# Reordering the first two head pairs of an attention and feed-forward kernel, and splitting its first loads

## The chip, the cores and the metric

One core of a Trainium2 chip runs the whole program. The metric is the time of one execution on the device in microseconds (us); the lower, the better. The core has a matrix engine (PE, with its weight loads, PEld), a vector engine (DVE), an activation engine (ACT), a general engine (POOL) and a queue engine (SP) that here does nothing but issue transfers. Transfers from HBM run on 16 DMA engines that all queues share.

## The reference

The inputs are q, k and v for 4 batches of 8 heads, 576 positions and 64 features. The reference adds two attentions and passes the result through two feed-forward blocks:

```python
q_d, k_d, v_d = means over groups of 4 positions        # 144 positions
out_up = repeat(softmax(q_d @ k_d.T / 8) @ v_d, 4)
scores = where(abs(i - j) < 4, q @ k.T / 8, -1e9)
x = out_up + softmax(scores) @ v                        # then (4, 576, 512)
xn = (x - mean(x)) / sqrt(var(x) + 1e-6) * g_ln
x = x + maximum(xn @ w_ch1, 0) @ w_ch2                  # 512 -> 2048 -> 512
xk, xr = mixes of x and x shifted by one position
out = sigmoid(xr @ w_r) * (square(maximum(xk @ w_k, 0)) @ w_v)
```

The weights reach the kernel as 64-bit words and are decoded to f32 on the core. Each product is made from three products of rounded halves (high by high, high by low, low by high).

## The kernel before

The 2304 tokens are cut into 6 chunks of 384. A chunk goes through attention (4 units, each of two heads), the norm, and the first feed-forward block. While PE runs the block of chunk c, the attention of chunk c+1 is fed in between by a budget. The second feed-forward block follows over all chunks. The change touches only the start: the attention of chunk 0 and the loading and decoding of the first weights.

**Chunk 0's attention** is done for two pairs of units at once. `pair(0)` and `pair(1)` are generators, and the string `FIRST` (L1339) is the order, written out by hand, in which their steps and a few others are emitted. Every instruction in it is held in program order on its engine. A `0` or `1` makes the next step of that pair. The steps of a pair are, in order:

1. sums of q and k over groups of four (DVE)
2. score products (PE, L861 and L868)
3. row maxima of the coarse scores (DVE, L879) and their exponentials (ACT, L884)
4. minimum with the mask, row maxima, subtraction (DVE, L887 to L889), exponential (ACT, L890)
5. row sums, reciprocals, scaling (DVE, L892 to L896)
6. transposes of the local part (DVE, L898) and scaling of the coarse part (ACT, L902)
7. copies of the transposed tile (L906: ACT; for the second pair two of them on DVE)
8. transposes of the coarse part (PE, L912), copies of them (ACT, L914), then `busy(IDLE)` for the first pair only
9. value products (PE, L923 and L930)
10. sum of the two attentions into x (ACT L939, DVE L940)
11. the mean over features (PE, L953)

The other letters: `a` and `b` are `value_sums` of the first and second pair (DVE, L792 and L794), which adds four loaded rows of v into one and is needed by step 9; `A`, `D`, `H` and `L` with a number decode and split that weight tile (A: two passes on ACT, L80 and L81; D: one on DVE, L83; H: the high half, ACT, L86; L: the low half, DVE, L89); `.` is `busy(1)` (L366), a matrix product whose result nobody uses; `W` is the same with `WARM` products (L360); `n` is the norm. After `FIRST`, `emit_first` (L680) makes the first four column blocks of the first layer, which needs weight tiles 0 and 1. Tiles 2 and 3 belong to the second layer. From tile 4 on, the planner orders the decoding.

**The loads** of the start are issued in program order: q and k of pair 0, q and k of pair 1 (some from ACT's queue), mask, vector; then `load_pair_v(0)` (L783) and `load_pair_vr(0)` (L788), the v windows and v rows of the first pair in one transfer each; then the first weight tile (L122: two transfers of 128 rows by 4 KB, 512 KB each); the coarse sums' first rows of the next units (L336, L337); the second pair's v rows, weight tile 1, the second pair's v windows, weight tile 2, q and k of the next two units (L313, L317), weight tile 3 and the next v (L322). Each later weight tile is asked for when an earlier one is decoded (step D). The program has eight semaphores for the transfers of SP and ACT together and takes them in turn, so that the ninth transfer in program order can be issued only when the first has landed, the tenth when the second has, and so on.

Of the kernel before, what the change touches and what calls it, by code (L numbers as in the profile page):

```python
# [22 lines left out]
NG = 4  # L23
# [4 lines left out]
KD = SD // 2  # L28
# [10 lines left out]
def tile_block(ctx: ExitStack, tc: tile.TileContext, qw, kw, kf, kr, vw, vr, vec, mask, w1, w2, wk, wv, wr, out):  # L39
    nc = tc.nc  # L40
# [27 lines left out]
    def in_order(on, ins):  # L68
        if on:
            tc.keep_in_program_order(ins)  # L70
# [5 lines left out]
    def decode(raw, pinned, ru):  # L76

        low, high = (raw.rearrange("p (n t) -> p n t", t=2)[:, :, i] for i in range(2))
        top = raw.bitcast(U8).rearrange("p (n t) -> p n t", t=8)[:, :, 3]
        in_order(pinned, nc.scalar.activation(ru.bitcast(F32), high.bitcast(F32), AF.Prelu, scale=-2.0 ** -80, alpha=-2.0 ** -32))  # L80
        in_order(True, nc.scalar.activation(low, top, AF.Copy, scale=1.0 / 32.0, bias=-31.0 / 64.0))  # L81
        yield ru.bitcast(F32)
        in_order(pinned, nc.vector.scalar_tensor_tensor(ru, ru, 3, low.bitcast(U32), op0=ALU.logical_shift_left, op1=ALU.bitwise_or))  # L83

    def split_hi(hi, w, vector=False):
        return nc.vector.tensor_copy(hi, w) if vector else nc.scalar.copy(hi, w)  # L86

    def split_lo(hi, lo, w):
        return nc.vector.tensor_tensor(lo, w, hi.bitcast(F32), op=ALU.subtract)  # L89

    def wtiles(nm):
        return [wpool.tile([128, 4, 512], F32R, tag="w", name=f"{nm}{t}") for t in "hl"]
# [7 lines left out]
    def pieces_w12():  # L100
        for p in range(3):
            yield from ((nm, p, k, 2) for nm in ("w1", "w2") for k in (0, 2))
        yield from ((nm, 3, k, 1) for nm in ("w1", "w2") for k in range(4))

    def conv_gen():
        keys = list(pieces_w12())
        late_keys = keys[-4:]
        raws, todo = {}, iter([(nm, p, k) for nm, p, k, _ in keys[:-4] if k % 2 == 0])

        def source(nm, p, k):  # L110
            return w1s[:, k, 1024 * p:1024 * p + 1024] if nm == "w1" else w2s[:, 4 * p + k, :]

        def fetch():
            key = next(todo, None)
            if key is None:
                return
            nm, p, k = key
            t = wpool.tile([128, 2, 1024], I32, tag="w", name="raw")
            raws[nm, p, k, 2] = t.rearrange("p k n -> p (k n)")
            for i in range(2):  # L120
                raws[nm, p, k + i, 1] = t[:, i]
                in_order(len(raws) < 12, nc.sync.dma_start(t[:, i], source(nm, p, k + i)))  # L122

        def fetch_late(key):
            if key in late_keys:
                t = raws[key] = stg.tile([128, 1024], I32, tag="stg", name="raw", bufs=RB)
                nc.sync.dma_start(t, source(*key[:3]))

        parts, got = {}, set()

        def step(op, n):

            if not 0 <= n < len(keys) or (op, n) in got:
                return
            got.add((op, n))
            pin = n < PINNED
            nm, p, k, m = keys[n]
            W = W1 if nm == "w1" else W2
            if op == "A":
                if p not in W:  # L140
                    W[p] = wtiles(f"{nm}_{p}")
                if m == 1:
                    rm = stg.tile([128, 2, 512], U32, tag="stg", name="rm", bufs=RB)[:, 0]
                elif k == 0:
                    parts["rm"] = wpool.tile([128, 2, 1024], U32, tag="w", name="rm")
                    rm = parts["rm"][:, 0]
                else:
                    rm = parts["rm"][:, 1]
                g = decode(raws[keys[n]], pin, rm)
                parts[n] = (g, next(g), *(t[:, k:k + m, :].rearrange("p k n -> p (k n)") for t in W[p]))  # L150
                return
            g, w, h, l = parts[n]
            if op == "D":
                next(g, None)
                if m == 2 or k % 2:
                    fetch()
                if n + 1 < len(keys):
                    fetch_late(keys[n + 1])
            elif op == "H":
                in_order(pin, split_hi(h, w, n in BY_VECTOR))  # L160
            else:
                in_order(pin, split_lo(h, l, w))
                done.update((nm, p, k + i) for i in range(m))

        for _ in range(AHEAD):
            fetch()
            yield
        yield step
        for n in range(len(keys) + 1):
            for ops in ((("H", n - 1), ("A", n)), (("L", n - 1), ("D", n))):  # L170
                if all(not 0 <= i < len(keys) or (op, i) in got for op, i in ops):
                    continue
                for op, i in ops:
                    step(op, i)
                yield
# [186 lines left out]
    def busy(n):  # L362

        for _ in range(n):
            bank = ps_at.tile([128, 512], F32, tag="sc", name="idle")
            in_order(True, nc.tensor.matmul(bank, ident, sets[0]["kf"][:, 0, 0:512], start=True, stop=True))  # L366
# [378 lines left out]
    def block(*parts):  # L745

        t = wpool.tile([128, 2048], F32, tag="w", name="first")
        n, views = 0, []
        for m in parts:
            views.append(t[:, n:n + m])  # L750
            n += m
        return views
# [9 lines left out]
    sets = [  # L762
        dict(q=q_0, kf=kf_0, qd=qd_0, v=v_0, Pd=pd_0, PdT=td_0, P=P_both, PT=pt_0, T=t_0),
        dict(q=q_1, kf=kf_1, qd=qd_1, v=v_1, Pd=pd_1, PdT=td_1, P=p_1.rearrange("p (g w) -> p g w", w=32), PT=pt_1, T=t_1),
    ]
# [14 lines left out]
            in_order(True, (nc.sync if pr else nc.scalar).dma_start(b["kf"][:, i], kf[0, 2 * pr + i]))  # L780

    def load_pair_v(pr):
        in_order(True, nc.sync.dma_start(sets[pr]["v"], vw[2 * pr:2 * pr + 2, :, 0:NG].rearrange("i p n h d -> p i n h d")))  # L783

    vr_01 = [block(2048)[0].rearrange("p (i r f) -> p i r f", i=2, r=4) for _ in range(2)]

    def load_pair_vr(pr):
        in_order(True, nc.sync.dma_start(vr_01[pr][0:KD].rearrange("p i r f -> p i (r f)"), vr[0, 2 * pr:2 * pr + 2].rearrange("i p r t d -> p i (r t d)")))  # L788

    def value_sums(pr):  # L790
        t = vr_01[pr][0:KD]
# [16 lines left out]
    nc.scalar.copy(ones_r, one)  # L808
    make_identity(nc, ident)
    load_pair_v(0)  # L810
    load_pair_vr(0)
    next(conv)
    for h in range(2):
        p = slice(64 * h, 64 * h + 64)
# [6 lines left out]
    for _ in zip(*[sums(*units[NHP + i]) for i in range(2)]):  # L821
        pass
    load_pair_vr(1)
    next(conv)
    load_pair_v(1)
    next(conv)
    for i in range(2):
# [13 lines left out]
    def pair(pr):  # L841
# [71 lines left out]
        for i in both:  # L913
            fixed(nc.scalar.copy(  # L914
                PdT[0:KD, i].rearrange("p t j (h m) -> p (t j) h m", h=2),
                tp[i].rearrange("p t j (h m) -> p (t j) h m", h=2)[:, :, :, 0:QB]))
        busy(0 if pr else IDLE)
        yield
# [37 lines left out]
    def first_norm():  # L956

        mean = means.pop(0)
        xc = xct[0] = pln.tile([128, KT, N], F32, tag="xc", name="xc")
        for k in range(KT):  # L960
            in_order(True, nc.vector.tensor_tensor(xc[:, k, :], xt[0][:, k, :], mean[:, 0:N], op=ALU.subtract))
        yield
        yield from split_x(0, True)
# [4 lines left out]
    steps = {"0": pair(0), "1": pair(1), "n": first_norm()}  # L968
    for o in FIRST.split():
        if o in "ab":  # L970
# [179 lines left out]
    def small(nm, tag="s", bufs=None):  # L1150
        return (right if tag == "k" else left)[-1].tile([128, N], F32, tag=tag, name=nm, bufs=bufs or SB)
# [94 lines left out]
    for s in range(NSC):  # L1246
# [28 lines left out]
        for j in range(2):  # L1275
            for o in range(KT):
                ps = bank()
                c = slice(128 * o, 128 * o + 128)
                n = slice(N * j, N * j + N)
                for k in range(KT):  # L1280
                    mm3(ps[:, 0:N], wr_t[0][:, k, c], wr_t[1][:, k, c], xh[:, k, n], xl[:, k, n], k == 0, k == KT - 1)
                t = small("r")
# [18 lines left out]
    for c in range(NCH):  # L1301
# [5 lines left out]
        for o in range(KT):  # L1307
# [6 lines left out]
            r = rins[c][o]  # L1314
# [21 lines left out]
PROB = 800  # L1336
PRO0 = 10
GAP = -1
FIRST = "0 0 1 1 0 0 1 . . A0 0 0 1 0 a 0 1 1 1 0 b 0 D0 1 H0 1 0 1 1 L0 A1 n n D1 H1 W n L1 A2 D2 H2 L2 A3 D3"  # L1339
EARLY = 44  # L1340
IDLE = 2
WARM = 8


# [55 lines left out]
```

## Time and profile before

| | |
|---|---|
| median of 3 runs | 749.43 us (748.63 to 751.29) |
| profiled execution: its time | 749.87 us |
| profiled execution: its span, first to last instruction | 748.1 us |
| PE busy | 733.1 us, 98% of the span |
| DVE, ACT, POOL busy | 439.1 us (59%), 374.5 us (50%), 106.5 us (14%) |
| bytes moved | 130.43 MB, 174 GB/s over the span |

The busy shares are means over stages. The start, some 100 us, has other limits than the rest: there DVE, ACT and the transfers are loaded as heavily as PE. The rows below are therefore taken from that stretch.

### The profile page before, as it was taken

The numbers are of one execution on the slowest core, as the hardware profiler recorded it, in microseconds if no ns is written. First come the engines' busy times: TensorE is split into PE (matmuls) and PEld (weight loads), VectorE is DVE, ScalarE is ACT, GpSimd is POOL, SyncE is SP. The second block draws the span as 40 slices with busy tenths as digits, with TensorE's granted clock in tenths as the row PEclk, the third lists the DMA queues.
The fourth block names the chain that finished last, engine by engine and source line by source line (L and its number), as shares of the span: only waits on it lengthen the run. The fifth ranks groups of instructions, "written<-read, shape, count | busy, mean of one in ns | idle before, by whom it ended". The sixth has DMA issues, their size and how long they took to land.

```text
span 748.1 us, 14134 instructions
## 1 busy us (share of the span) xinstructions
PE 733.1 (98%) x5548; PEld 707.5 (95%) x5548; DVE 439.1 (59%) x820; ACT 374.5 (50%) x781; POOL 106.5 (14%) x141
## 2 busy tenths in 40 slices
PE   6899999999999999999999999999999999999997
PEld 5598899999999999999999999999999999999997
DVE  5889977755475657555766455447997266233211
ACT  2798884653353543444454444236987476311100
POOL 3431203200164205410300030002000000000000
PEclk9999999999999999999999999999999999999999
DMA  8999552646366745754432247807725637785311
GB/s 266 263 345 361 108 172 76 173 139 204 100 172 159 184 142 141 193 159 129 137 122 93 77 142 271 292 29 262 236 83 188 221 103 301 259 281 168 109 67 47
DMA packets 75354, 130.43 MB, mean 174 GB/s; under 512 B 8376, under 2 KB 51896, under 8 KB 73624
## 3 DMA queue, kind: packets, MB, share of 16 engines
q1 hardware_dynamic: 64792, 119.57, 48.8%
q0 software_dynamic: 9920, 9.25, 6.9%
q8 instruction: 43, 0.70, 0.4%
q10 hardware_dynamic: 576, 0.72, 0.3%
q14 instruction: 23, 0.19, 0.1%
HBM read 89.13 MB, written 40.37 MB: 173 GB/s over the span
## 4 chain that ended last, share of the span: by engine, by line
PE 89%; DMA 8%; ACT 1%; DVE 0%; issue 0%; SPq 0%; ACTq 0%
PE b_ps L1189 12%; PE acc L291 9%; PE h_ps L291 9%; PE acc L292 8%; PE acc L293 8%; PE h_ps L292 8%; PE h_ps L293 8%; PE b_ps L291 7%; PE b_ps L293 7%; PE b_ps L292 7%; DMA raw<-in_w 3%; PE av L476 2%; DMA q<-in_qw 2%; DMA first<-in_vr 2%; PE sc L404 1%; DMA v<-in_vw 1%
## 5 line engine op out<-in xcount | busy, mean ns | idle before, releaser
L670 ACT ACTIVATE hh<-h_ps 128x384 fp32r<-128x384 f32 x96 | 47.0, 489 | 102.9 <-PE h_ps L293 101.1
L671 DVE SCALAR_TENSOR_TENSOR hl<-h_ps,hh 128x384 fp32r<-128x384 f32 x96 | 53.1, 553 | 76.8 <-ACT hh L670 76.2
L1189 PE MATMUL b_ps<-xk,wk 128*128 128x384 f32 x504 | 87.9, 334 | 0.0
L1189 PEld LDWEIGHTS b_ps<-xk,wk 128*128 128x128 f32 x504 | 87.5, 188 | 0.0
L713 POOL TENSOR_TENSOR x<-x2t,x 128x384 f32<-128x384 f32 x24 | 24.1, 1020 | 291.1 <-DVE x2t L712 290.9
L291 PE MATMUL b_ps<-ko,wv 128*128 128x384 f32 x192 | 64.1, 334 | 0.0
L293 PE MATMUL b_ps<-ko,wv 128*128 128x384 f32 x192 | 64.1, 334 | 0.0
L292 PE MATMUL b_ps<-ko,wv 128*128 128x384 f32 x192 | 64.1, 334 | 0.0
L1315 DVE TENSOR_TENSOR rin<-b_ps,rin 128x384 f32<-128x384 f32 x24 | 13.3, 557 | 61.9 <-PE b_ps L293 61.1
L336 POOL DMA_DIRECT2D kd<-in_kr x36 | 35.3, 982 | 85.4 <-DMA kd<-in_kr 76.1
L337 POOL DMA_DIRECT2D vd<-in_vr x36 | 37.8, 1054 | 17.7 <-DMA vd<-in_vr 16.1
L83 DVE SCALAR_TENSOR_TENSOR rm<-rm,raw 128x512 uint32<-128x512 uint32 (+1 forms) x40 | 33.7, 841 | 6.2 <-ACT raw L81 6.0
L1241 ACT CAST ko<-kin 128x1536 fp32r<-128x1536 f32 x12 | 17.6, 1475 | 38.9 <-PE b_ps L292 23.3
L80 ACT ACTIVATE rm<-raw 128x512 f32<-128x512 f32 (+1 forms) x40 | 32.5, 811 | 8.0 <-DMA raw<-in_w 6.5
L292 PEld LDWEIGHTS b_ps<-ko,wv 128*128 128x128 f32 x192 | 36.0, 188 | 0.0
L291 PEld LDWEIGHTS b_ps<-ko,wv 128*128 128x128 f32 x192 | 36.0, 188 | 0.0
L293 PEld LDWEIGHTS b_ps<-ko,wv 128*128 128x128 f32 x192 | 36.0, 188 | 0.0
L1243 DVE TENSOR_TENSOR ko<-kin,ko 128x1536 fp32r<-128x1536 f32 x12 | 20.9, 1754 | 22.6 <-ACT ko L1241 22.6
L291 PE MATMUL h_ps<-ah,w_2h 128*128 128x384 f32 x96 | 33.5, 349 | 0.0
L292 PE MATMUL acc<-hl,w_1h 128*128 128x384 f32 x96 | 32.4, 337 | 0.6 <-DVE hl L671 0.6
L291 PE MATMUL h_ps<-ah,w_3h 128*128 128x384 f32 x96 | 32.8, 342 | 0.0
L291 PE MATMUL h_ps<-ah,w_1h 128*128 128x384 f32 x96 | 32.8, 342 | 0.0
(227 smaller groups left out, 2081.3 us busy)
## 6 DMA issues: line engine op xcount, KB each, us to landing
raw<-in_w SPq DMA_DIRECT2D x32, 512.0 KB, 9.8
kd<-k SPq DMA_DIRECT2D x48, 192.0 KB, 2.1
kin<-kd SPq DMA_DIRECT2D x12, 768.0 KB, 6.9
wk<-wkd SPq DMA_DIRECT2D x7, 1024.0 KB, 8.0
v<-in_vw SPq DMA_DIRECT2D x20, 256.0 KB, 3.4
rd<-r SPq DMA_DIRECT2D x24, 192.0 KB, 1.8
rin<-rd SPq DMA_DIRECT2D x24, 192.0 KB, 2.5
out<-rin SPq DMA_DIRECT2D x24, 192.0 KB, 3.2
```

Source lines behind the costliest of these rows:

```text
L80: in_order(pinned, nc.scalar.activation(ru.bitcast(F32), high.bitcast(F32), AF.Prelu, scale=-2.0 ** -80, alpha=-2.0 ** -32))
L83: in_order(pinned, nc.vector.scalar_tensor_tensor(ru, ru, 3, low.bitcast(U32), op0=ALU.logical_shift_left, op1=ALU.bitwise_or))
L291: nc.tensor.matmul(ps, wh, ah, start=first, stop=False)
L292: nc.tensor.matmul(ps, wh, al, start=False, stop=False)
L293: nc.tensor.matmul(ps, wl, ah, start=False, stop=last)
L336: in_order(r > 0, eng.dma_start(kd, kr[b, hp, r], **op))
L337: in_order(r > 0, eng.dma_start(vd, vr[b, hp, :, r], **op))
L670: nc.scalar.activation(hh, ps[:, 0:N], AF.Relu)
L671: last_hl[0] = nc.vector.scalar_tensor_tensor(hl, ps[:, 0:N], 0.0, hh.bitcast(F32), op0=ALU.max, op1=ALU.subtract)
L713: nc.gpsimd.tensor_tensor(x[:, o, :], t, x[:, o, :], op=ALU.add)
L1189: nc.tensor.matmul(ps, a, m[:, k, :], start=start and k + i == 0, stop=k == nk - 1 and i == 2, skip_group_check=True)
L1243: nc.vector.tensor_tensor(l, t[g], h.bitcast(F32), op=ALU.subtract)
```

## The change

Value sums of the first pair (`a`) now come before the second pair's minimum and no longer behind it; those of the second pair (`b`) come after weight tile 0's step D instead of before it. The first pair's steps 5, 6 and 7 are emitted before the second pair's step 4, and the first decoding step `A0` moves behind the second pair's step 4 and the first pair's step 8. The two `.` are gone, and `IDLE` is 0 instead of 2, so that four unused products on PE disappear; `W` stays. The v windows and v rows are loaded in one transfer per unit instead of one per pair. The weight tiles 0, 1 and 2 come in four transfers of 64 rows each (256 KB) instead of two of 128 rows; the later ones stay as they were. No computed value changes.

```diff
-                in_order(len(raws) < 12, nc.sync.dma_start(t[:, i], source(nm, p, k + i)))
+                early = len(raws) < 10
+                for h in range(2 if early else 1):
+                    rows = slice(64 * h, 64 * h + 64) if early else slice(0, 128)
+                    in_order(len(raws) < 12, nc.sync.dma_start(t[rows, i], source(nm, p, k + i)[rows]))
...
     def load_pair_v(pr):
-        in_order(True, nc.sync.dma_start(sets[pr]["v"], vw[2 * pr:2 * pr + 2, :, 0:NG].rearrange("i p n h d -> p i n h d")))
+        for i in range(2):
+            in_order(True, nc.sync.dma_start(sets[pr]["v"][:, i], vw[2 * pr + i, :, 0:NG]))
...
     def load_pair_vr(pr):
-        in_order(True, nc.sync.dma_start(vr_01[pr][0:KD].rearrange("p i r f -> p i (r f)"), vr[0, 2 * pr:2 * pr + 2].rearrange("i p r t d -> p i (r t d)")))
+        for i in range(2):
+            in_order(True, nc.sync.dma_start(vr_01[pr][0:KD, i].rearrange("p r f -> p (r f)"), vr[0, 2 * pr + i].rearrange("p r t d -> p (r t d)")))
...
-FIRST = "0 0 1 1 0 0 1 . . A0 0 0 1 0 a 0 1 1 1 0 b 0 D0 1 H0 1 0 1 1 L0 A1 n n D1 H1 W n L1 A2 D2 H2 L2 A3 D3"
+FIRST = "0 0 1 1 0 0 1 0 0 0 a 1 0 A0 1 1 1 0 D0 1 b 0 H0 1 0 1 1 L0 A1 n n D1 H1 W n L1 A2 D2 H2 L2 A3 D3"
 EARLY = 44
-IDLE = 2
+IDLE = 0
```

## Rows read from the trace of the kernel before

**Rows 1.** Chain that ended last, in order of time: start, us, what.

```profile
0.74 4.39 DMA first<-in_qw
...
5.57 11.27 DMA first<-in_vr
...
47.28 8.98 DMA raw<-in_w
...
56.35 1.17 ACT rm L80
...
62.42 0.44 PE acc L292
```

**Rows 2.** Busy time by window: PE, PEld, DVE, ACT, POOL; PEclk, DMA share, GB/s.

```profile
37.00:100.00 63.00, 60.45 (x499) 55.62 (x498) 55.61 (x97) 55.62 (x98) 14.04 (x16) 1.00 0.83 258
100.00:420.00 320.00, 319.97 (x2658) 308.17 (x2659) 199.61 (x450) 154.06 (x390) 67.17 (x80) 1.00 0.52 146
```

**Rows 3.** Timeline of ACT: start, us, engine, line; in brackets idle before, releaser.

```profile
20.84 1.15 ACT L80 ACTIVATE rm<-raw 128x1024 f32<-128x1024 f32 x1 [5.08 <-DMA raw<-in_w]
...
22.89 1.33 ACT L902 ACTIVATE first<-first,mx 128x144 f32<-128x144 f32 x4
24.12 0.61 ACT L890 ACTIVATE first<-first 128x480 f32<-128x480 f32 x1
24.61 2.05 ACT L906 COPY first<-first 32x384 f32<-32x384 f32 x4
```

**Rows 4.** Timeline of DVE around the second pair's minimum and both value sums.

```profile
18.78 0.72 DVE L887 TENSOR_TENSOR first<-sc,mask_t 128x240 f32<-128x240 f32 x2 [2.23 <-PE sc L868]
...
20.80 1.21 DVE L792 TENSOR_TENSOR first<-first 72x1024 f32<-72x1024 f32 x1
...
24.82 0.67 DVE L892 TENSOR_REDUCE sm<-first 128x16 f32<-128x496 f32 x1 [2.02 <-ACT first L890]
...
28.22 1.22 DVE L792 TENSOR_TENSOR first<-first 72x1024 f32<-72x1024 f32 x1
...
35.75 1.95 DVE L961 TENSOR_TENSOR xc<-x,mean 128x384 f32<-128x384 f32 x4
```

**Rows 5.** Timeline of PE in the same stretch.

```profile
18.19 0.45 PE L868 MATMUL sc<-first 64*32 64x30 f32 x26 [4.53 <-issue]
18.57 4.07 PE L366 MATMUL idle<-first,ident 128*128 128x512 f32 x4
...
24.64 2.21 PE L366 MATMUL idle<-first,ident 128*128 128x512 f32 x4
...
31.07 0.88 PE L923 MATMUL av<-first 128*64 128x96 f32 x16 [0.60 <-ACT first L914]
...
37.40 1.86 PE L680 MATMUL h_ps<-ah,w_0h 128*128 128x384 f32 x8
```

**Rows 6.** Windows again, columns as in Rows 2: loads of the start.

```profile
11.00:13.00 2.00, 2.00 (x63) 1.77 (x65) 1.87 (x4) 1.42 (x8) 0.00 (x0) 1.00 1.05 232
17.00:22.00 5.00, 3.75 (x30) 1.31 (x29) 3.15 (x5) 1.17 (x2) 0.62 (x1) 0.50 1.00 231
25.00:27.00 2.00, 1.78 (x4) 0.30 (x2) 1.90 (x6) 1.94 (x5) 0.12 (x1) 1.00 1.08 372
...
33.00:35.00 2.00, 1.96 (x12) 0.96 (x9) 1.46 (x3) 2.00 (x5) 1.76 (x2) 1.00 0.74 143
```

**Rows 7.** Timeline of ACT at weight tiles 5 (its first row) and 7.

```profile
50.45 1.15 ACT L80 ACTIVATE rm<-raw 128x1024 f32<-128x1024 f32 x1
51.51 1.03 ACT L86 CAST w_1h<-rm 128x1024 fp32r<-128x1024 f32 x1
...
56.35 1.17 ACT L80 ACTIVATE rm<-raw 128x1024 f32<-128x1024 f32 x1 [0.29 <-DMA raw<-in_w]
```

**Rows 8.** Timeline of SP: two issues, eight transfers apart in the queue.

```profile
41.44 0.33 SPq L122 DMA_DIRECT2D raw<-in_w  x1
...
50.38 0.33 SPq L122 DMA_DIRECT2D raw<-in_w  x1
```

## The prediction

> **What bounds the kernel now.** I first read the windows to find where PE, the busiest engine, is idle. From 100 to 420 us it is busy 319.97 of 320 us, and it works through all chunks in order, so whatever the start gains or loses before 100 us stays to the end. From 37 to 100 us PE is busy 60.45 of 63 us, but so, in effect, are ACT and DVE (55.62 and 55.61) and the DMA engines (share 0.83) [rows 2]. PE's real work starts with `emit_first` at 37.40 us [rows 5]. The question is what sets that point, and whether an earlier start survives until 100 us.
>
> Before 37 us I read ACT, DVE and PE side by side. ACT sits idle for 5.08 us and starts tile 0's decode at 20.84, when the second half of the tile has landed; this decode and the first pair's scaling (from 22.89) stand ahead of the second pair's exponential, which therefore starts only at 24.12 [rows 3]. DVE, having made the second pair's minimum from 18.78 on, does the first value sums at 20.80, then idles 2.02 us until that exponential is there [rows 4]. PE has an idle stretch of its own: 4.53 us until 18.19, ended by nothing the profile names, in the middle of the second pair's scores [rows 5].
>
> The chain that ended last tells another story for the same time: six transfers in a row from 0.74 to 56.27 us (three in the middle are not shown), each issued when the one before in the chain landed; then ACT's decode of tile 7, DVE, and PE at 62.42 [rows 1]. In the program's order these are the 1st, 10th, 18th, 26th, 34th and 42nd transfer of SP and ACT; the step of eight is the turn of the eight semaphores. So the loads are a second, parallel bound: they are always full, and the weight tiles arrive when the queue has moved what stands ahead of them. Tile 7 lands at 56.27 and ACT, idle 0.29 us, starts it at 56.35 [rows 1, 7]. For tile 5, the transfer issued at 41.44 frees the eighth after it at 50.38 [rows 8], and ACT starts the tile at 50.45 [rows 7]. Slack: 0.1 us at either.
>
> **The edits to the order.** The first pair's sums and transposes end before DVE's idle stretch of 2.23 us ahead of 18.78 [rows 4]. Value sums `a` move into it. They took from 20.80 to the end of the work before the 2.02 us of idle, 24.82 - 2.02 - 20.80 = 2.0 us [rows 4]. They must wait for the first pair's v rows, which land at 5.57 + 11.27 = 16.84 [rows 1], so they end at about 18.85, and the minimum behind them starts 0.1 us later than now. Queued behind them on DVE are the minimum, maximum and subtraction of pair 1; if the rows land later, all of these do. Bounds: the rows go out in two transfers now, so 0 to 1 us later.
>
> The second pair's exponential needs DVE's subtraction, ready at 20.8 + 0.1. ACT is then free: from 15.8 on (20.84 - 5.08) it does the first pair's scaling, 1.33 us, and its four copies, 2.05 us [rows 3], done by 19.3. So the exponential goes from 24.12 to about 20.95: 3.2 us earlier. DVE's list from there to the norm's first subtraction at 35.75 holds the same work as now, and its idle of 2.02 us is gone. Two new waits may lie in it. D0 comes after A0, whose two passes (20.84 to 22.89, 2.05 us [rows 3]) now follow the exponential (0.61 us) and the first pair's two copies and end near 24.6; DVE reaches D0 at about 25.0: no wait. Then `b` needs the second pair's rows, which now it does at 28.22 without waiting [rows 4], and after the change at about 26: 0 to 2 us, I take 0, since the rows stand early in the queue. **Start of PE's real work: 37.40 - 3.2 = 34.2 us.**
>
> The four unused products leave PE. [...]
>
> **The edits to the loads.** Bytes and their order in the queue stay. Ten transfers more go out, each 0.33 us of SP's time [rows 8], 3.3 us spread over 25 us in which SP mostly waits for landings: hidden; without that cover it would be 3.3 us. But ten more take a turn among the eight semaphores. Tile 3's first half is issued when three quarters of tile 2 have landed instead of half of it: 256 KB more, 0.7 us at 372 GB/s or 1.1 at 231 [rows 6], in the stretch (33 to 35 us) where the DMA engines are already at 0.74 and 143 GB/s [rows 6]. Cost 0 to 1.1; I take 0.5, since all later tiles queue behind it.
>
> What halves of 64 rows do is not in the trace. The nearest rows are the v rows, transfers of 72 partitions: while they are in flight (11 to 13 and 17 to 22 us) the DMA engines are as full as ever (1.05, 1.00) yet move 232 and 231 GB/s; with 128-partition loads (25 to 27) 372 [rows 6]. Three tiles are 3.146 MB: 13.6 us at 231 against 8.5 at 372. So the cost lies between 0, if neighbouring halves overlap, and 5.2 us. I take 1.0, near the low end: halves of both kinds are in the queue at once.
>
> [...]
>
> **What is late next, and the sum.** With everything up to PE's start 2.7 us earlier (3.2 - 0.5), tile 5 still lands at 50.4 and tile 7 at 56.3. ACT works in order, so it stands at these two decodes as before. What remains of the gain is work that the planner puts ahead of the waiting decode, such as the cast at 51.51, 1.03 us [rows 7]: 0 to 2.7; I take 0.7. Against it stand the loads: 0.5 + 1.0. Sum: -0.7 + 0.5 + 1.0 = +0.8, from 749.87 to 750.7 for a profiled execution. The profiled one is 0.44 above the median of 749.43, so **750.2 us**, which is no change: about 0.3% (2.2 us) is what a measurement of this kernel can tell from none.
>
> **The rivals.**
> Gain reaches the end: the planner reorders ACT's work from tile 4 on, the halves cost nothing, and tile 5's decode chain, which now shares ACT and DVE with other work, runs straight after its landing. For it: PE has idle time of only 2.55 us between 37 and 100, so an earlier start is an earlier end if tiles keep up. Against it: 0.1 us of slack at tiles 5 and 7. Time: 749.43 - 3.2 = 746.2.
> Slower, by the halves: each 64-row transfer runs at the 231 GB/s of the v rows, and 5.2 us are added ahead of tile 3. It decides once the loss exceeds the 0.7 gained and the 2.2 of the bound, that is from half of its price. For it: the windows above; against: those loads have 72 rows, and 33 to 35 us shows engines with time to spare. Time: 749.43 + 5.2 + 0.5 - 0.7 = 754.4.
> The change doesn't do what it says: the v rows land late and hold DVE, or PE stays at the lower clock, and `emit_first` starts near 37 as now. Then only the loads count: 749.43 + 1.5 = 750.9, again no change.
>
> **How the numbers follow.** Gain swallowed by the loads, within 2.2 us: 0.42. Gain reaches the end: 0.26. Halves: 0.24. No gain at the start: 0.08. Faster by over 0.3% is the second case, 0.26; slower the third, 0.24; the rest, 0.50, is the same. The range reaches from the second case's time to the third's, 746.2 to 754.4; the likeliest case alone spans 748.0 to 751.6.
>
> **What would show it.** In the changed profile: ACT's idle before A0 gone and the second pair's exponential near 21; value sums right ahead of the minimum, which starts near 18.9; `emit_first` near 34.2; ACT idle in front of tile 4 and tile 5, released by their landings at 50.4 to 52; the window of tiles 0 to 2 nearer to 231 than to 372 GB/s if the halves cost. I am wrong if tile 5's decode starts before 50 us, which means that the loads were not full, or if PE's idle time from its start to 100 us doesn't grow beyond 2.55 us while the start is earlier.

## The result and the profile after

| | before | after |
|---|---|---|
| median | 750.18 us (748.63 to 751.29) | 755.12 us (754.21 to 756.28) |
| span of the profiled execution | 748.1 us | 752.4 us |
| start of `emit_first` on PE | 37.40 us | 42.32 us |
| ACT's decode of weight tile 5 | 50.45 us | 55.87 us |

The median of before is that of four runs here; the one that the prediction started from, 749.43, was that of three. The ratio is 1.0068, 95% interval 1.0046 to 1.009: the changed kernel is slower by some 5 us, and tile 7's decode at 61 us is already 5 us late. Line numbers of after are higher by 3 to 5.

Windows of after, the first four those of [rows 6], the last two those of [rows 2]: busy time of PE, PEld, DVE, ACT, POOL, then PEclk, DMA share, GB/s.

```profile
11.00:13.00 2.00, 2.00 (x25) 1.78 (x25) 1.60 (x4) 1.45 (x8) 0.00 (x0) 1.00 1.04 160
17.00:22.00 5.00, 2.17 (x34) 1.60 (x33) 3.20 (x7) 2.57 (x7) 0.94 (x2) 1.00 0.91 193
25.00:27.00 2.00, 2.00 (x29) 2.00 (x27) 1.83 (x5) 2.00 (x5) 0.00 (x0) 1.00 1.07 238
33.00:35.00 2.00, 1.42 (x18) 1.45 (x20) 0.00 (x0) 0.00 (x0) 1.31 (x2) 0.50 1.00 229
...
37.00:100.00 63.00, 61.52 (x474) 55.39 (x471) 56.78 (x97) 54.29 (x93) 14.08 (x16) 0.98 0.88 270
100.00:420.00 320.00, 319.64 (x2678) 307.41 (x2677) 200.97 (x453) 155.49 (x394) 67.44 (x80) 1.00 0.51 146
```

Read the last two columns together. The DMA engines are as busy as before (1.07 from 25 to 27 us, before 1.08), and move 238 GB/s where [rows 6] show 372. The engines are not idle; each byte costs them more (the median 4 KB packet of that window took 262 ns, in before 171). From 33 to 35 us neither ACT nor DVE does anything at all.

Timeline of PE, after (idle before, and what ended it, in brackets):

```profile
19.83 0.44 PE L873 MATMUL sc<-first 64*32 64x30 f32 x26 [5.30 <-issue]
...
33.58 1.55 PE L928 MATMUL av<-first 128*64 128x96 f32 x16 [4.20 <-DMA first<-in_vw]
...
42.32 1.84 PE L683 MATMUL h_ps<-ah,w_0h 128*128 128x384 f32 x8
```

The second pair's value products, which started at 31.07 in [rows 5] behind ACT, now wait 4.20 us for the v windows of that pair. Behind this wait the granted clock of PE is 0.50 (33 to 35 us; 1.00 there in before [rows 6]). DVE and ACT, after:

```profile
16.74 1.18 DVE L797 TENSOR_TENSOR first<-first 72x1024 f32<-72x1024 f32 x1
...
20.41 0.72 DVE L892 TENSOR_TENSOR first<-sc,mask_t 128x240 f32<-128x240 f32 x2 [1.70 <-PE sc L873]
...
26.65 1.22 DVE L83 SCALAR_TENSOR_TENSOR rm<-rm,raw 128x1024 uint32<-128x1024 uint32 x1
27.79 1.21 DVE L797 TENSOR_TENSOR first<-first 72x1024 f32<-72x1024 f32 x1
```

```profile
22.55 0.60 ACT L895 ACTIVATE first<-first 128x480 f32<-128x480 f32 x1 [2.94 <-DVE first L894]
...
52.49 1.14 ACT L80 ACTIVATE rm<-raw 128x1024 f32<-128x1024 f32 x1 [0.62 <-DMA raw<-in_w]
...
55.87 1.13 ACT L80 ACTIVATE rm<-raw 128x1024 f32<-128x1024 f32 x1
...
61.34 1.19 ACT L80 ACTIVATE rm<-raw 128x1024 f32<-128x1024 f32 x1
```

The order edit does its work: the sums of the first pair (16.74) stand in front of the minimum (20.41), those of the second (27.79) behind D0 (26.65), and the exponential moved from 24.12 [rows 3] to 22.55. But tile 4 is waited for (0.62 us), tile 5 starts 5.4 us later than in [rows 7] and tile 7, at 61.34, 5.0 us later. The chain that ended last (start, us, what) tells it from the side of the transfers:

```profile
8.26 7.71 DMA raw<-in_w
15.99 8.94 DMA first<-in_vr
24.94 11.27 DMA raw<-in_w
36.23 6.98 DMA kz<-in_kw
43.22 9.16 DMA raw<-in_w
```

As in [rows 1] each transfer starts when the one eight places ahead has landed. The last landing in it is now at 43.22 + 9.16 = 52.38 and belongs to tile 4; ACT takes it up at 52.49.

### The profile page after: what moved, and what is told of

Same layout as the page of the kernel before. It is cut to its first block, busy times and chain, and to the rows that moved or that the text cites. A ratio compares the mean times of both kernels' runs of the same rounds, so it can differ in the third digit from the quotient of the medians.

```text
span 752.4 us, 14139 instructions
## 1 busy us (share of the span) xinstructions
PE 733.4 (97%) x5540; PEld 711.6 (95%) x5540; DVE 439.6 (58%) x820; ACT 374.6 (50%) x781; POOL 106.2 (14%) x141
## 4 chain that ended last, share of the span: by engine, by line
PE 87%; DMA 8%; DVE 2%; ACT 2%; issue 1%; SPq 0%; ACTq 0%
PE b_ps L1194 12%; PE acc L294 8%; PE h_ps L294 8%; PE acc L295 8%; PE acc L296 8%; PE h_ps L295 8%; PE h_ps L296 8%; PE b_ps L295 7%; PE b_ps L294 7%; PE b_ps L296 7%; DMA raw<-in_w 4%; PE av L479 2%; PE sc L407 1%; DMA first<-in_vr 1%; PE scd L403 1%; PE av L488 1%
## 5 line engine op out<-in xcount | busy, mean ns | idle before, releaser
L340 POOL DMA_DIRECT2D vd<-in_vr x36 | 39.7, 1103 | 27.9 <-DMA vd<-in_vr 23.2
L294 PE MATMUL h_ps<-ah,w_2h 128*128 128x384 f32 x96 | 33.5, 349 | 0.0
L294 PE MATMUL acc<-hh,w_1h 128*128 128x384 f32 x96 | 32.7, 351 | 0.0
```

What stands on the lines that cost most here:

```text
L294: nc.tensor.matmul(ps, wh, ah, start=first, stop=False)
L340: in_order(r > 0, eng.dma_start(vd, vr[b, hp, :, r], **op))
```

## The experiments

Time is given as the ratio to the kernel before on the same chip, with its 95% interval.

**The halves alone, added to before.**

```diff
-                in_order(len(raws) < 12, nc.sync.dma_start(t[:, i], source(nm, p, k + i)))
+                early = len(raws) < 10
+                for h in range(2 if early else 1):
+                    rows = slice(64 * h, 64 * h + 64) if early else slice(0, 128)
+                    in_order(len(raws) < 12, nc.sync.dma_start(t[rows, i], source(nm, p, k + i)[rows]))
```

> The kernel before with one part of the change alone: weight tiles 0 to 2 in halves of 64 rows; order, unused products and v loads as before. Theory P: the full cost of the halves, 4 to 5 us, 754 to 755.5 us. Theory T: six more turns, 2 to 3 us, about 752.5. Theory C: no change, 750.

Measured: 1.0083 [1.0065, 1.0101], median 755.42 us. PE and ACT of that kernel:

```profile
33.87 1.55 PE L926 MATMUL av<-first 128*64 128x96 f32 x16 [4.73 <-DMA first<-in_vw]
...
42.57 1.86 PE L683 MATMUL h_ps<-ah,w_0h 128*128 128x384 f32 x8
```

```profile
55.44 1.12 ACT L80 ACTIVATE rm<-raw 128x1024 f32<-128x1024 f32 x1
```

With the old order, the old unused products and v by pair, this one edit makes the same picture as the whole change: the wait for the v windows, `emit_first` at 42.57, tile 5 at 55.44. It alone is enough for the loss.

**The change without the halves, and with another form of split.** The first kernel is the change with raw tiles of 128 rows again (the diff above taken back). The second keeps the change's number of transfers and their 256 KB, but cuts columns instead of rows:

```diff
-                    rows = slice(64 * h, 64 * h + 64) if early else slice(0, 128)
-                    in_order(len(raws) < 12, nc.sync.dma_start(t[rows, i], source(nm, p, k + i)[rows]))
+                    part = slice(512 * h, 512 * h + 512) if early else slice(0, 1024)
+                    in_order(len(raws) < 12, nc.sync.dma_start(t[:, i, part], source(nm, p, k + i)[:, part]))
```

> The changed kernel with one edit undone: weight tiles 0 to 2 come again in two transfers of 128 rows. Theory P (transfers of 64 rows move at some 230 GB/s instead of 370, because of the rows they cover): the 5 us come back and the order's gain shows a little, 748 to 750 us; 4 KB packets of the raw tiles take about 165 ns again. Theory T (the turn of eight semaphores: ten more transfers leave less in flight): six of the ten extra transfers are gone, so some 60% of the loss comes back, about 752. Theory C (PE stays at its lower clock because the unused products are gone): 754 to 755, nothing comes back.

> The changed kernel with the first three weight tiles still in twice as many transfers of 256 KB, but each of 128 rows by 2 KB instead of 64 rows by 4 KB: same number of turns, same bytes, other rows. Theory P: as fast as with 128-row transfers of 512 KB, 748 to 751 us. Theory T: as slow as the changed kernel, 754 to 756. Theory C: 754 to 755.

Measured: 128 rows 1.0002 [0.9983, 1.002], columns 0.9986 [0.9969, 1.0003]. Between columns and halves only the shape of twelve early transfers differs, and the ratios differ by 0.82%, some 6 us; between 128 rows and halves it is 0.66%, some 5 us. From 7 to 38 us the median 4 KB packet took 292 ns in after and 173 with 128 rows. So the extra transfers and their turns among the semaphores are not the cause; the 64 rows are. The start of PE's work and ACT's rows of 128 rows, then of columns:

```profile
33.47 1.86 PE L680 MATMUL h_ps<-ah,w_0h 128*128 128x384 f32 x8
...
48.03 1.15 ACT L80 ACTIVATE rm<-raw 128x1024 f32<-128x1024 f32 x1 [0.26 <-DMA raw<-in_w]
```

```profile
34.12 1.87 PE L683 MATMUL h_ps<-ah,w_0h 128*128 128x384 f32 x8
...
46.56 1.12 ACT L80 ACTIVATE rm<-raw 128x1024 f32<-128x1024 f32 x1 [2.86 <-DMA raw<-in_w]
49.89 1.13 ACT L80 ACTIVATE rm<-raw 128x1024 f32<-128x1024 f32 x1
```

`emit_first` starts 3.3 to 3.9 us before that of [rows 5], and the time is that of before. With columns ACT stands idle 2.86 us at tile 4 and starts tile 5 at 49.89, 0.6 us earlier than before [rows 7]; with 128 rows it starts tile 5 2.4 us earlier.

**The forms of load by themselves.** A kernel that computes nothing loads six pieces in one form, waits for them with a vector copy, and goes on to the next form. In a first one, one store of the output fell into each of the first four phases; the second stores first.

```python
for n in range(6):
    load(slice(0, 64), n)          # one phase; the others: (64, 128), (32, 96), two halves, ...
tc.keep_in_program_order(nc.vector.tensor_copy(s, T[:, :, 0:1024:64]))
```

> The disputed cost by itself: this kernel leaves out the whole computation and only loads the weights' raw rows, 4 KB a row, in seven phases one after the other, with one copy on DVE between them: six transfers of 128 rows (3.15 MB); the same bytes as twelve halves of rows 0 to 63 and 64 to 127; as twelve of 128 rows by 2 KB; six of rows 0 to 63 (1.57 MB); six of rows 32 to 95 (1.57 MB); eighteen of rows 0 to 31, 32 to 95 and 96 to 127 (3.15 MB); and the first again. Theory P (which rows a transfer covers decides): 128 rows 8 to 10 us, halves 14 to 15, columns 8 to 10, rows 0 to 63 7 to 8, rows 32 to 95 4 to 5, the three-part form 11 to 13. Theory S (64-row transfers are slow because each engine gets half as many rows, whichever they are): rows 32 to 95 as slow as rows 0 to 63, 7 to 8, and the three-part form slower than the halves. If halves take 8 to 10 us here, neither: then the cost needs the other traffic of the kernel.

> The computation is left out: after its four stores of zeros the kernel only loads, six times in each of eight phases, a tile of 128 rows by 4 KB (or a part of it), and a vector copy ends each phase. Two theories of why halves are slow. P, which rows: rows 0 to 63 and rows 64 to 127 each reach their share of the memory at half the rate, rows 32 to 95 reach it at the full rate. S, how few: a transfer of 64 rows gives each DMA engine fewer rows and is slow whichever rows it has. Both expect for 3.146 MB in one form: 128 rows 10 to 11 us, halves 15 to 16.5, columns (two transfers of 128 rows by 2 KB) 10.5 to 12. For half the bytes: P expects rows 0 to 63 and rows 64 to 127 at 8.5 to 10.5 us alike, with 4 KB packets near 300 ns, and rows 32 to 95 at 6 to 7 us with packets near 160; S expects 8.5 to 10.5 for all three. Rows 0 to 31, 32 to 95 and 96 to 127 as three transfers: P between 12 and 16.5, since two of the three stay within a few rows; S 16 or more.

Measured, the second one's timeline of DVE; the number in brackets is the length of a phase. The order is 128 rows, halves, columns, rows 0 to 63, rows 64 to 127, rows 32 to 95, three parts, 128 rows:

```profile
35.29 0.27 DVE L89 COPY s<-T 128x96 int32<-128x96 int32 x1 [10.55 <-DMA T<-in_w]
51.97 0.27 DVE L89 COPY s<-T 128x96 int32<-128x96 int32 x1 [16.41 <-DMA T<-in_w]
65.06 0.27 DVE L89 COPY s<-T 128x96 int32<-128x96 int32 x1 [12.82 <-DMA T<-in_w]
75.22 0.27 DVE L89 COPY s<-T 128x96 int32<-128x96 int32 x1 [9.90 <-DMA T<-in_w]
85.28 0.27 DVE L89 COPY s<-T 128x96 int32<-128x96 int32 x1 [9.79 <-DMA T<-in_w]
93.65 0.27 DVE L89 COPY s<-T 128x96 int32<-128x96 int32 x1 [8.11 <-DMA T<-in_w]
110.39 0.27 DVE L89 COPY s<-T 128x96 int32<-128x96 int32 x1 [16.47 <-DMA T<-in_w]
121.57 0.27 DVE L89 COPY s<-T 128x96 int32<-128x96 int32 x1 [10.92 <-DMA T<-in_w]
```

The same 3.146 MB take 10.55 us as 128 rows and 16.41 us as halves, with both kinds of half in the queue: 5.9 us more. A phase also holds the time before its first packet and after its last. Counted between these, 128 rows took 9.1 us, both halves 13.9, either half alone 7.7 and 7.6, rows 32 to 95 6.1. So neighbouring halves hardly overlap: 13.9 us together, 15.3 one after the other. Rows 0 to 63 alone need 9.90 us for half the bytes, nearly the time of a whole load (10.55), and rows 64 to 127 need 9.79. The median 4 KB packet took 159 ns with 128 rows, 315 with either half alone (289 with both queued), 159 with rows 32 to 95. So in these loads it is which rows, as theory P has it, and not how few; why, isn't shown.

P's time for rows 32 to 95 (6 to 7 us for the phase) was missed: 8.11. Its DMA engines were busy for a share of 0.60, against 0.82 with 128 rows, and what kept them idle isn't shown. Columns (12.82, expected 10.5 to 12) cost 2.3 us against whole tiles here and nothing that can be measured in the kernel. The three parts lie within what both theories expected and decide nothing. The first kernel gave the same lengths within 0.8 us from its second phase on (halves 16.36, rows 32 to 95 8.42, three parts 16.34); they were longer than what had been expected of it.

**The order alone, and v by unit alone.** Before with the new `FIRST` and `IDLE = 0`, and before with only the v windows and rows by unit (the second and third part of the change's diff).

> The kernel before with the new order and without the unused products, all loads as before. Theories P and T: the second pair's value products wait for its v windows, which land at 30.9 us as before, so the start gains little; 748.5 to 750.5 us. Theory C: the lower clock alone costs the 5 us, 754 to 755.

> The kernel before with one part of the change alone: v windows and v rows loaded by unit. Theory L (the landing of weight tiles 4 to 7 sets the end of the start, and with it the time; the loads by unit bring these landings forward by 2 us or so): tile 5's decode starts near 48 to 49 instead of 50.4, time 747 to 749. If the loads by unit do nothing: 750, tile 5 at 50 to 51.

Measured: order 0.9998 [0.9979, 1.0016], v by unit 0.9989 [0.9969, 1.0009]. PE of the order alone:

```profile
32.12 1.55 PE L923 MATMUL av<-first 128*64 128x96 f32 x16 [3.45 <-DMA first<-in_vw]
...
39.63 1.85 PE L680 MATMUL h_ps<-ah,w_0h 128*128 128x384 f32 x8
```

and of v by unit alone, with ACT's tile 5:

```profile
29.12 0.88 PE L925 MATMUL av<-first 128*64 128x96 f32 x16
...
35.29 1.85 PE L680 MATMUL h_ps<-ah,w_0h 128*128 128x384 f32 x8
```

```profile
48.13 1.11 ACT L80 ACTIVATE rm<-raw 128x1024 f32<-128x1024 f32 x1
```

The order alone brings PE to the second pair's value products before their v windows have landed; it waits 3.45 us, and PE's real work starts later than before, not earlier. The transfers by unit bring those windows and everything behind them forward: 29.12 instead of 31.07, tile 5 at 48.13 instead of 50.45. Together they make the start of 33.5 us that the kernel with 128 rows shows. None of the three moves the time by an amount that can be measured (each interval is some 1.4 us wide to either side): the start of `emit_first` went to 39.63, 35.29 and 33.47 us, with ratios of 0.9998, 0.9989 and 1.0002.

**The clock.** Columns, with two of the unused products back behind the first pair's copies:

```diff
-FIRST = "0 0 1 1 0 0 1 0 0 0 a 1 0 A0 ...
+FIRST = "0 0 1 1 0 0 1 0 0 0 a 1 0 . . A0 ...
```

> The changed kernel with the first tiles in columns (128 rows), and two unused products, four instructions on PE, put back behind the first pair's transposes. Theory L: PE's real work starts near 34 as without them and waits for tiles later; 748 to 749.5, no change against the same kernel without them. Theory C (the lower clock costs time): value products at the higher clock, start 1 to 2 us earlier and the time with it, 746 to 747.

Measured: 1.0002 [0.9984, 1.0021], against 0.9986 [0.9969, 1.0003] without them. Windows of the kernel without, then with them:

```profile
17.00:37.00 20.00, 17.24 (x167) 14.05 (x167) 18.09 (x33) 16.45 (x32) 8.93 (x10) 0.74 1.04 272
```

```profile
17.00:37.00 20.00, 16.61 (x158) 11.71 (x158) 16.84 (x32) 15.32 (x32) 9.18 (x11) 0.91 1.02 276
```

PE of the kernel with them:

```profile
28.76 1.00 PE L928 MATMUL av<-first 128*64 128x96 f32 x16 [1.80 <-DMA first<-in_vw]
...
36.38 1.85 PE L683 MATMUL h_ps<-ah,w_0h 128*128 128x384 f32 x8
```

The granted clock goes from 0.74 to 0.91 and the time does not fall. `emit_first` started at 36.38 us, 2.3 later than without, where both theories had expected 34 or earlier, and tile 5 at 49.92 as without (49.89). It is no clean test of the clock: in the profiled execution the first pair's exponential is already 1.0 us later, ahead of the products, and PE waits 1.80 us for the v windows.

**Fewer bytes in the queue.** Columns, without the adding loads of the coarse sums of chunk 1 (three of the four rows of k and v are left out of these sums; 24 transfers of 72 KB, twelve of them issued before 40 us):

```diff
-        for r in range(4):
+        for r in range(1 if c == 1 else 4):
```

> The changed kernel with the first tiles in columns, and with the three rounds of accumulating loads from POOL for the first units of chunk 1 left out (twelve small transfers, 0.9 MB; the coarse sums of those units are then those of every fourth position only). Theory L: tiles 4 to 7 land 1.5 to 3 us earlier, ACT's wait for tile 4 (2.86 us) goes, and the time falls by as much, to 745.5 to 747. Theory A (ACT's and DVE's own work from tile 2 on is the bound): tiles land earlier but their decode does not start earlier, 748 as with them.

Measured: 0.9942 [0.9924, 0.996]. Windows, PE and ACT:

```profile
17.00:37.00 20.00, 16.93 (x145) 14.10 (x144) 18.32 (x35) 16.79 (x32) 0.00 (x0) 0.75 1.04 335
```

```profile
16.41 0.33 PE L873 MATMUL sc<-first 64*32 64x30 f32 x26 [3.46 <-issue]
...
33.45 1.86 PE L683 MATMUL h_ps<-ah,w_0h 128*128 128x384 f32 x8
```

```profile
46.30 1.17 ACT L80 ACTIVATE rm<-raw 128x1024 f32<-128x1024 f32 x1
```

The time (median 745.22 us, a little below the expected 745.5 to 747) is 0.6% below before and 0.44%, some 3.3 us, below columns (0.9986). Against columns `emit_first` starts 0.7 us earlier, ACT's wait at tile 4 is gone, and tile 5 is started at 46.30 instead of 49.89, 3.6 us earlier. That fits the landings as what sets the end of this stretch with columns. It doesn't show it: the edit also takes away the adding loads between 40 and 84 us. And against 128 rows, with the same start (33.47), tile 5 is 1.7 us earlier and the time shorter by 0.6%, some 4.5 us, which is more than that landing explains. The kernel is a measurement and no candidate, since part of the sums is missing.

**The loads in another order.** The change with 128 rows, and the loads of q, k and v for chunk 1's first units moved behind the fetches of tiles 4 and 5 (two letters in `FIRST`, after `D0` and `D1`):

```diff
-    for i in range(2):
-        load_qk(*units[NHP + i], True)
...
-    load_v(*units[NHP])
...
-... D0 1 b 0 H0 1 0 1 1 L0 A1 n n D1 H1 W ...
+... D0 q 1 b 0 H0 1 0 1 1 L0 A1 n n D1 r H1 W ...
```

> The change with raw tiles of 128 rows, and the loads of q, k and v for chunk 1's first units moved from behind tile 2 to behind the fetches of tiles 4 and 5. If the landings of the weight tiles set the time (theory L), tiles 3 to 5 land 1 to 2.5 us earlier than in the change with 128 rows (tile 5's decode from 48.0 to 45.5 to 47), and the time goes from 748.6 to 746 to 747.5, unless PE has to wait for those q and k in chunk 1's attention. If the start of PE's work sets the time (theory S), that start stays near 33.5 us and the time stays at 748 to 749.

Measured: 0.9987 [0.9971, 1.0004], the same as before. ACT and a window of that kernel:

```profile
46.46 1.17 ACT L80 ACTIVATE rm<-raw 128x1024 f32<-128x1024 f32 x1
...
50.57 1.15 ACT L80 ACTIVATE rm<-raw 128x1024 f32<-128x1024 f32 x1 [0.60 <-DMA raw<-in_w]
54.11 1.14 ACT L80 ACTIVATE rm<-raw 128x1024 f32<-128x1024 f32 x1 [1.32 <-DMA raw<-in_w]
```

```profile
50.00:60.00 10.00, 8.24 (x73) 6.98 (x72) 7.46 (x14) 7.19 (x13) 2.57 (x3) 1.00 1.07 373
```

Tile 5 is started at 46.46 instead of 48.03, as expected, but the moved loads now stand ahead of tiles 6 and 7: ACT waits 0.60 and 1.32 us for them, tile 7 starts at 54.11 instead of 53.59, and PE is busy 8.24 of the 10 us from 50 to 60 (9.54 with 128 rows). The expected 746 to 747.5 us were missed: an earlier tile 5 alone gave nothing that can be measured. No version with all of the sums beat the kernel before by an amount that can be measured.

## Why the prediction was wrong

**The step that failed** is the term for the halves: 1.0 us, from a range of 0 to 5.2, with the reason that halves of both kinds are in the queue at once. The cost was named and its price was about right: in the kernel the halves cost 6.2 us (0.83%) alone, some 6 against columns and some 5 against 128 rows; by themselves they cost 4.8 us from first to last packet and 5.9 with the ends of the phase. The windows of [rows 6] gave 5.2. The place within the range was wrong. The reason was an argument without a row, against rows that showed full DMA engines moving 231 GB/s; with both halves queued, the loads alone moved 3.146 MB in 13.9 us from first to last packet, 226 GB/s, where 128 rows moved them at 346 GB/s.

It is the rival "slower, by the halves" that happened (754.4). With 5.9 in place of 1.0 the sum would have been 749.43 - 0.7 + 0.5 + 5.9 = 755.1. That this is the measured median is luck in part: no run shows the 0.7 or the 0.5 in it. The median lies 0.7 us above the range, and the median of before rose as much with its fourth run; as a difference, the 4.9 us between the two medians are those of the rival (5.0).

**The steps of the order** held wherever the halves were gone. Forecast, then measured with 128 rows: minimum at 18.85 (18.53), second pair's exponential at 20.95 (20.67), D0 at 25.0 without a wait (24.77), `b` near 26 without a wait (25.91), `emit_first` at 34.2 (33.47; with columns 34.12). The first two, with 128 rows:

```profile
18.53 0.72 DVE L889 TENSOR_TENSOR first<-sc,mask_t 128x240 f32<-128x240 f32 x2
```

```profile
20.67 0.60 ACT L892 ACTIVATE first<-first 128x480 f32<-128x480 f32 x1 [1.30 <-DVE first L891]
```

In after itself the minimum waits 1.70 us for scores behind PE's idle time, and `emit_first` is 8.1 us later than forecast.

**A wait that was missing** is that of the second pair's value products for their v windows. The rows of before show them starting at 31.07 behind ACT; that their v windows had only just landed was not looked at (SP issues the transfer eight behind them at 30.95). Moving the steps ahead of them by 3 us turns the landing into the limit (3.45 us with the order alone). The loads by unit, which I costed at 0 to 1 us on the wrong side, take that wait away. Without the halves the two errors cancel, so that the forecast start came out right by luck.

**"The loads swallow the gain"** is shown in part. It held with columns: a start 3.3 us earlier, ACT idle at tile 4, tile 5 only 0.6 us earlier, the same time. With 128 rows it did not hold as written: the start is 3.9 us earlier, tile 5 (48.03) and tile 7 (53.59) are still 2.4 and 2.8 us earlier than in [rows 7], and the time is the same within 1.5 us. Windows with 128 rows:

```profile
17.00:37.00 20.00, 17.30 (x171) 14.46 (x171) 18.54 (x35) 16.77 (x33) 9.02 (x10) 0.76 1.06 290
37.00:100.00 63.00, 59.72 (x525) 54.82 (x523) 54.55 (x96) 53.98 (x97) 12.30 (x14) 1.00 0.81 251
```

PE's idle time from 37 to 100 us grew from 2.55 to 3.28 us, so that only 0.7 of the 3.9 us are lost there. The profiled execution is 1.7 us shorter than that of before (span 746.4 against 748.1), but the ratio shows no gain. v by unit alone looks the same: tile 5 2.3 us earlier, a span of 745.3, no gain in the ratio. Whether the scatter of the executions hides a gain here, or where it goes, isn't shown. One of my tests failed in the kernel with 128 rows: tile 5 starts before 50 us, and I had written that this would mean that the loads were not full. They were (the DMA share is 1.06 from 17 to 37 us); the transfers by unit had brought them forward.

**The clock.** No run shows the 0.5 us that the forecast takes off the 3.2 (to 2.7) for PE's clock. Bringing two products back raised the granted clock from 0.74 to 0.91 (17 to 37 us) and gained nothing that can be measured, in a run that is no clean test. In after a granted clock of 0.50 shows behind the wait for the v windows: the work from the second pair's value products up to `W` takes from 33.58 to 40.18, 6.6 us, where the granted clock is 0.50 until 39 us; with 128 rows the same work takes 4.2 us (27.18 to 31.35) at 1.00. With the halves alone, which keep all the unused products, it is 6.6 us too. So some 2.4 us of the late start come with the wait, and not with the products that were taken out; what they are worth at the end isn't shown. **The extra turns of the semaphores**, 0.5 us, could not be seen: columns have the same number.

What is left open: the times of one kernel lie up to 6 us apart, so that gains and losses under some 1.5 us (v by unit, columns, the clock) are not told apart here.

## What to carry to other kernels

When the DMA engines show a full share, look at the GB/s beside it. Here the share was the same (1.07 and 1.08 from 25 to 27 us) at 238 and 372 GB/s, and the form of the transfers was the cost: those that covered only the lower or only the upper 64 rows, even with the neighbour queued (16.41 against 10.55 us for the same bytes). Before an engine's start is moved forward, list the landing time of every tile that its steps read, not only of those that are waited for now. And where a start is moved ahead of a queue that is full, the gain can end at that queue, as with columns here (ACT idle for 2.86 us at tile 4); what shortened the time (0.9942) was fewer loads in it.

## What was not expected of the hardware

In the kernel of loads alone, with only one form in flight, the median 4 KB packet took 315 ns when the transfer covered rows 0 to 63 or 64 to 127, and 159 ns for 128 rows and for rows 32 to 95.

The loads that add to their destination weighed more here than their bytes: without them (ten transfers of 72 KB are issued between 17 and 37 us with columns) the full queue moved 335 instead of 272 GB/s in these 20 us, at the same share of 1.04. In before, from 7 to 38 us, the median packet of 576 bytes took 68 ns in POOL's queue, which adds, and 29 in the queue of SP, which doesn't; whether the adding or the queue makes the difference isn't shown.

PE's idle time in the second pair's scores, ended by nothing that the profile names, is 4.53 us before [rows 5], 5.30 after, 5.72 with the order alone and 3.46 without the adding loads. In all ten traces of the whole kernel a packet of 16 KB that the profile calls "instruction" starts between 13.88 and 17.16 us, and the scores go on 1.4 to 1.8 us after it has ended, early or late as it is. PE may be waiting for that packet there; what it holds, whether PE waits for it and what delays it isn't shown.
